# Own gate rows for the second chunk, four row transfers per later chunk, and a larger count for each junk matmul

## The chip, the cores and the metric

One core of one Trainium2 chip runs the whole program. The metric is the device time of one execution in microseconds (us). The kernel before took 325.11 us in the median of 3 runs (324.2 to 326.46). One more execution was recorded by the hardware profiler; it took 324.24 us by the same metric.

Engines are named as the profile names them: PE is the matmul engine (TensorE), PEld its weight loads, DVE is VectorE, ACT is ScalarE, POOL is GpSimd, SP is SyncE, which here only issues transfers. Each engine works through its own queue in order.

## What is computed

Three layers, one after another, on 2 batches of 768 steps. The first is a gated recurrent attention with 8 heads of 40 values, then a gated MLP that mixes along the sequence, then a channel mix.

```python
# 1: mLSTM, per batch b and head h, steps t = 0..767
m_new  = max(f[t] + m, i[t])
f_stab = exp(f[t] + m - m_new); i_stab = exp(i[t] - m_new); m = m_new
C = f_stab * C + i_stab * outer(v[t], k[t]);   n = f_stab * n + i_stab * k[t]
y[t] = sigmoid(o[t]) * (C @ q[t]) / max(|n . q[t]|, 1)
# 2: gMLP on x = y, 320 wide
h = relu(x @ w_in); u, v = h[:512], h[512:]
v_n = (v - mean(v)) / sqrt(var(v) + 1e-6)
x = (u * (w_spatial @ v_n + b_spatial)) @ w_out
# 3: channel mix on x, with xk, xr blends of x and x one step back
out = sigmoid(xr @ w_r) * (relu(xk @ w_k)**2 @ w_v)
```

## The kernel before

The recurrence is computed in chunks of 128 steps, 6 chunks in each of 2 batches, so 12 positions. `SEQ` orders them chunk by chunk: positions 0 and 1 are the first chunk of the two batches, 2 and 3 the second chunk, 4 and 5 the third, and so on. In text below "position 2" means the loop round p=2 as well as its chunk; the names of tasks stand in `position(p)` (L882 to L966).

For one position PE makes: the scores of q and k for both halves of the heads (`sc`, L458, task S0), the log decay matrix of each half (`ld`, tasks S0 and S1), the product of the earlier state with q (`ip`, L560, task I), the state update (`sp`, L526, task T), the weighted sum of values for each half (`av`, L580, tasks N0 and N1), and the turn of the result into columns (`tp`, L628, task X). ACT takes the exponential of `ld`, DVE multiplies it by the scores (`dt`), and DVE, POOL and ACT bring the result out as `x` and split it into a high and a low part (`xg`). The state update needs the weighted keys `kw` (POOL, L510), which need the position's key and value tile `kvq`.

Once a position is turned, its share of the gMLP's input product is queued as fillers: 8 matmuls of `vp` each (with `w_v`), and 32 of `up` (with `w_u`) for each pair of chunks of one batch. Fillers are a first-in, first-out list (`fill`, L781): if the head waits for its weights, nothing behind it is taken. The fillers of the first pair, positions 0 and 2, must be through before position 5 is turned, as only three `xg` tiles are kept (L621 to L623). `vp` goes through a normalisation chain (L717 to L723): relu on ACT, statistics on DVE, a root made of four small POOL operations (L712 to L715), the scaling on ACT (L722), then a high part on ACT and a low part on POOL (`vn`). The spatial mix (`spp`) reads all `vn`, and from there on come `wop`, `kp`, `rp` and `vv`.

**Gates.** The decays need running maxima `mg` and sums over each chunk. The first chunk's are computed at the start from the gate rows as they arrive, 16 rows of (batch, head) (`gate_set("a", 16, ...)`, L384 to L408, ten small operations; its tiles are `Lxa` and `Axa`). The remaining maxima are one scan of 640 columns (L810, called at L823). For all chunks together, `mg` and the gates are loaded again as 96 rows (`late_rows`, L836), the ten operations run on these (`gate_set("c", 96, ...)`, L847), and a task G at position 1 turns the result (`gpsc`, L415) and makes the state decays. The chunk sums are then moved by transfers into the operands `lt` and `rl` of the decay matmul (`gate_rows`, L421): 2 + 4 + 4 transfers for each chunk from the second on, the second chunk's at position 0. The first chunk's `ld` is made otherwise: `first_logd` (L462) uses `Lxa` and `Axa` where they lie, with six matmuls (L466, L468 four times, L470) instead of `ld` (L488) and its mask (L490).

**The order.** The program order of PE, ACT, DVE and POOL is laid down by a planner in the kernel while it is built: `clock[0]` is its time for PE, `free[...]` those of the other engines, chains are lists of (engine, cost, operation), and `load` keeps a due time for each transfer (230 KB per us up to 20 us, 360 after, plus 1.8 us). Where the next task isn't due, PE is given fillers, and where there is none, junk matmuls (`heat`, L350, tile `wp`), each counted at 0.107 us. So a planned wait becomes a fixed number of matmuls, whatever the chip does. Transfers are issued by SP in program order.

**Weights.** `w_in` comes in two halves, v and u, of three parts of 512 KB each, as 64-bit words, and is turned into two 32-bit tiles by a chain for each part (`widen`, L251: L273, L277, L281 on DVE, L272 and L289 on ACT, L233 on POOL). The v half is loaded before the loop. The u half is loaded whole at the end of position 0 (L940) and its chains are queued at position 1 (L889).

**Output gates.** ACT applies the sigmoid to the output gates of chunks 2 to 5 in task S1 of position 3 (L929); each change between sigmoid and exponential loads a table.

## Time and profile before

| | us |
|---|---|
| median of 3 runs (lowest, highest) | 325.11 (324.2, 326.46) |
| the profiled execution, same metric | 324.24 |
| its span from first to last instruction | 322.5 |
| mean granted TensorE clock, share of full speed | 0.993 |
| PE busy in the span | 308.0 |

A busy engine is one with an instruction under way; junk matmuls count as busy. Durations below are from the profiled execution. Its time stands 1.74 us above its span, and 0.87 us below the median of the timed runs. A row of the timeline gives start, duration, engine, line, operation, tile written and tiles read, shape and count; in brackets stands the idle time before it and what ended that.

### The profile page before, as it was taken

To read this page: it belongs to the slowest core of one execution; us is meant where nothing else is said; L and a number is where in the kernel's file an instruction comes from. 1 tells how busy PE (TensorE), PEld (TensorE's weight loads), DVE (VectorE), ACT (ScalarE), POOL (GpSimd) and SP (SyncE) were. 2 spreads that over 40 slices of the span, in tenths; PEclk is the share of its full clock that TensorE was granted. 3 is DMA by queue.
4 is the path that set the end of the run, shared out by engine and by line. 5 is a ranking of instruction groups with operands and counts; after the bars stand their busy time and mean duration, and the time that the engine had idled before them with its cause. 6 is when DMAs were issued, how large, how long until landed. Compare 5 with 4: busy or idle time off the path is not lost.

```text
span 322.5 us, 5694 instructions
## 1 busy us (share of the span) xinstructions
PE 308.0 (95%) x2075; PEld 286.9 (89%) x2075; DVE 211.3 (66%) x412; ACT 170.3 (53%) x354; POOL 155.0 (48%) x211
## 2 busy tenths in 40 slices
PE   7999989699999999977999999999999999999995
PEld 5866776689998998977999999999999999999995
DVE  7594496665655644463788998989866765645611
ACT  3631366754466555286334465476883754743610
POOL 5242167573575865377356652746722702502600
PEclk9999999899999999999999999999999999999999
DMA  6932946333424212204702520331101001001001
GB/s 164 294 87 80 321 140 192 109 109 104 152 87 153 92 31 69 89 25 130 229 20 74 170 86 24 92 114 40 42 2 62 0 22 41 2 20 41 2 20 41
DMA packets 14162, 28.78 MB, mean 89 GB/s; under 512 B 2567, under 2 KB 8007, under 8 KB 14135
## 3 DMA queue, kind: packets, MB, share of 16 engines
q1 hardware_dynamic: 14103, 28.37, 28.3%
q8 instruction: 16, 0.26, 0.3%
q0 software_dynamic: 32, 0.07, 0.1%
q14 instruction: 11, 0.09, 0.1%
HBM read 26.20 MB, written 1.97 MB: 87 GB/s over the span
## 4 chain that ended last, share of the span: by engine, by line
PE 77%; POOL 7%; DMA 5%; ACT 4%; DVE 3%; SPq 2%; issue 1%; DVEq 0%; POOLq 0%
PE spp L653 15%; PE kp L653 14%; PE vv L653 13%; PE wop L653 7%; PE wp L355 5%; PE vp L653 5%; PE rp L653 4%; PE up L653 4%; PE av L580 3%; PE sc L458 3%; DMA w_inv<-in_w_in_dram 2%; POOL vn L233 2%; PE ld L488 2%; SPq L214 2%; DMA kvq<-in_kvq_dram 1%
## 5 line engine op out<-in xcount | busy, mean ns | idle before, releaser
L1159 POOL TENSOR_TENSOR sq<-sq 128x384 f32<-128x384 f32 x32 | 29.9, 942 | 47.9 <-ACT sq L1158 47.8
L653 PE MATMUL spp<-wsp,vn 128*128 128x384 f32 x288 | 51.0, 335 | 1.7 <-POOL vn L233 1.3
L653 PEld LDWEIGHTS spp<-wsp,vn 128*128 128x128 f32 x288 | 49.8, 188 | 2.4 <-POOL vn L233 1.6
L653 PE MATMUL kp<-xk,wk 128*128 128x384 f32 x256 | 45.3, 334 | 0.0
L653 PEld LDWEIGHTS kp<-xk,wk 128*128 128x128 f32 x256 | 44.5, 188 | 0.0
L653 PE MATMUL vv<-wv,k 128*128 128x320 f32 x288 | 42.9, 309 | 0.0
L653 PEld LDWEIGHTS vv<-wv,k 128*128 128x128 f32 x288 | 42.4, 188 | 0.0
L233 DVE TENSOR_TENSOR k<-sq,k 128x384 fp32r<-128x384 f32 x32 | 26.1, 819 | 13.6 <-ACT k L1160 13.6
L653 PE MATMUL up<-xg,w_u 128*128 128x256 f32 x192 | 30.5, 293 | 2.3 <-ACT vr L718 1.4
L1056 POOL TENSOR_TENSOR vs<-vs,u 128x384 f32<-128x384 f32 x16 | 19.5, 1222 | 19.5 <-DVE vs L1055 18.1
L653 PEld LDWEIGHTS up<-xg,w_u 128*128 128x128 f32 x192 | 25.8, 191 | 3.4 <-ACT vr L718 1.6
L653 PE MATMUL vp<-w_v,xg 128*128 128x512 f32 x96 | 28.4, 411 | 0.0
L277 DVE SCALAR_TENSOR_TENSOR wbits<-wsq,wbits 128x320 int32<-128x320 int32 (+1 forms) x27 | 22.2, 822 | 8.7 <-ACT wsq L272 8.4
L580 PEld LDWEIGHTS av<-kvq,dt 128*128 128x128 f32 x192 | 25.2, 199 | 1.4 <-issue 0.3
L580 PE MATMUL av<-kvq,dt 128*128 128x123 f32 (+1 forms) x192 | 25.7, 279 | 0.3 <-DMA kvq<-in_kvq_dram 0.2
L1158 ACT ACTIVATE sq<-kp 128x384 f32<-128x384 f32 x32 | 15.5, 489 | 16.8 <-PE kp L653 14.8
L653 PE MATMUL wop<-gt,wo 128*128 128x384 f32 x128 | 22.8, 334 | 0.0
L653 PEld LDWEIGHTS wop<-gt,wo 128*128 128x128 f32 x128 | 22.2, 188 | 0.0
L501 DVE TENSOR_TENSOR dt<-dt,sc 128x512 f32<-128x512 f32 x20 | 13.6, 682 | 11.7 <-POOL dt L499 6.0
L233 POOL TENSOR_TENSOR vn<-vr,vn 128x512 fp32r<-128x512 f32 x12 | 16.3, 1355 | 7.3 <-ACT vn L723 7.3
L498 ACT ACTIVATE dt<-ld 128x512 f32<-128x512 f32 x20 | 11.9, 597 | 14.7 <-PE ld L490 7.6
L653 PEld LDWEIGHTS vp<-w_v,xg 128*128 128x128 f32 x96 | 17.3, 189 | 2.6
(160 smaller groups left out, 575.6 us busy)
## 6 DMA issues: line engine op xcount, KB each, us to landing
kvq<-in_kvq_dram SPq DMA_DIRECT2D x10, 516.0 KB
qk<-in_qk_dram SPq DMA_DIRECT2D x24, 160.0 KB
wraw<-in_w_k_dram SPq DMA_DIRECT2D x6, 512.0 KB
wraw<-in_w_v_dram SPq DMA_DIRECT2D x8, 320.0 KB
wraw<-in_w_sp_dram SPq DMA_DIRECT2D x12, 192.0 KB
og<-in_o_tok_dram SPq DMA_DIRECT2D x12, 160.0 KB
out_dram<-ob SPq DMA_DIRECT2D x12, 160.0 KB
w_inv<-in_w_in_dram SPq DMA_DIRECT2D x3, 512.0 KB
```

Source lines behind the costliest of these rows:

```text
L214: sync.dma_start(out=out, in_=in_)
L233: eng.tensor_tensor(out=out, in0=a, in1=b.bitcast(F32), op=ALU.subtract)
L277: vec.scalar_tensor_tensor(out=t["bits"], in0=t["sq"].bitcast(I32), scalar=3, in1=t["bits"], op0=ALU.logical_shift_left, op1=ALU.bitwise_or)
L355: pe.matmul(wp[:, :256], junk[:, :P], junk, start=True, stop=True)
L458: pe.matmul(st["sc", i, x][:, h * P:(h + 1) * P], k_[64 * x:64 * x + D, h, :], q_[64 * x:64 * x + D, h, :], start=True, stop=True)
L498: ("A", 0.48, lambda: act.activation(out=d2, in_=ld, func=AF.Exp), ("e", i, hh)),
L501: ("V", 0.6, lambda: vec.tensor_tensor(out=d2, in0=d2, in1=sc, op=ALU.mult)))
L580: pe.matmul(av[:, own_, :], A[:, h, :], vt[:, own_, :], start=True, stop=True)
L653: pe.matmul(out[0], l, x, start=j == 0, stop=j == len(prs) - 1)
L1056: ("P", 1.29, lambda: pool.tensor_tensor(out=vs, in0=vs, in1=ut[b][:, d, sl], op=ALU.mult)),
L1158: chain(("k2", g, f), ("A", 0.49, lambda: act.activation(out=sq, in_=ps, func=AF.Relu), ("kp", g, f)), ("P", 0.96, lambda: pool.tensor_ten ...
L1159: ("P", 0.96, lambda: pool.tensor_tensor(out=sq, in0=sq, in1=sq, op=ALU.mult)),
```

## The change

- The second chunk gets a gate set of its own on the 16 rows as they lie (`gate_set("b", 16, ...)`), and its `ld` is made by `first_logd` as the first chunk's. The scan is cut in three: the first chunk, the second, and the last four (512 columns).
- The 96-row set is loaded and computed later: its loads come after the q and k of position 2, its chain is due from 20 us at the earliest, and task G moves from position 1 to position 2. A new task B at position 0 turns the second chunk's gates.
- `gate_rows` begins with the third chunk, at position 2. It makes 2 + 2 transfers for each chunk instead of 2 + 4 + 4; odd and even chunks use different rows of `rl`, and both halves are written at once, in task S0.
- A junk matmul in a wait is counted at 0.187 us instead of 0.107.
- The u half of `w_in` is loaded one part at each of positions 0, 1 and 2, and its chains are queued at position 3.
- For positions from the sixth on, the normalisation leaves out two of the four POOL operations and scales on DVE instead of ACT.
- The transfers ahead of the loop are put in another order: position 1's `kvq` before the second part of the v half, the q and k of position 2 before the late rows.

```diff
     def idle_to(t):
         while warm[0] and clock[0] < t - 0.1:
             heat(1)
+            clock[0] += 0.08
             advance(clock[0])
...
-    first_ = {k: gp.tile([P, P], F32R, name=k + "xa") for k in "LA"}
+    first_ = {(k, nm): gp.tile([P, P], F32R, name=k + "x" + nm) for nm in "ab" for k in "LA"}
...
-            for first, sign in ((-16, 1), (17, -1)):
+            for first, sign in ((-16 - 4 * j, 1), (17 + 4 * j, -1)):
...
-    def gate_rows(c, hh):
-
+    def gate_rows(c):
         finish(("G1", 0), stall=False)
         after = done["G1", 0]
         L, A = [G1[k][c:96:NCH] for k in "LA"]
-        if hh == 0:
-            for b in range(B):
-                load(lts[c % 2][:16, b].bitcast(F32), A[8 * b:8 * b + 8].rearrange("h w t -> h (w t)").bitcast(F32), 8, after)
+        for b in range(B):
+            load(lts[c % 2][:16, b].bitcast(F32), A[8 * b:8 * b + 8].rearrange("h w t -> h (w t)").bitcast(F32), 8, after)
         for w in range(2):
-            for b in range(B):
-                r = 16 + 2 * b + w
-                e = load(rl[r:r + 1, 512 * hh:512 * hh + 512].bitcast(F32),
-                         L[8 * b + 4 * hh:8 * b + 4 * hh + 4, w].bitcast(F32), 2, after)
+            r = 16 + 4 * (c % 2) + w
+            e = load(rl[r:r + 3:2, :].bitcast(F32), L[:, w].bitcast(F32), 8, after)
...
     def egate(b, c, w):
-        if c < 1:
+        if c < 2:
             return GC[c]["eg"][:, w, 8 * b:8 * b + 8]
...
     def logd(i, hh):
         b, c = divmod(i, NCH)
-        if c == 0:
+        if c < 2:
+            if ("A", i, hh) not in st:
+                first_logd(i, hh)
             sc = st.pop(("sc", i, hh))
...
-        early = SEQ.index(i) < 4
-        pe.matmul(ld, lts[c % 2][:, b], rl[:, hh * 512:(hh + 1) * 512], start=True, stop=not early)
-        if early:
-            pe.matmul(ld, mask[:, 1], mask[:, 0:1].to_broadcast([P, 4, P]), start=False, stop=True)
-            clock[0] += 0.21
+        pe.matmul(ld, lts[c % 2][:, b], rl[:, hh * 512:(hh + 1) * 512], start=True, stop=True)
...
+            early = SEQ.index(i) < 5
+
             def root():
                 pool.tensor_tensor(out=sb[:, 8:9], in0=sb[:, 7:8], in1=eps[:, 0:1], op=ALU.add)
                 pool.tensor_tensor(out=sb[:, 8:9], in0=sb[:, 8:9], in1=eps[:, 1:2], op=ALU.pow)
+                if not early:
+                    return
...
-                  ("P", 1.2, root),
-                  ("A", 0.6, lambda: act.activation(out=vr, in_=vr, func=AF.Identity, scale=sb[:, 8:9], bias=sb[:, 9:10])),
+                  ("P", 1.2 if early else 0.75, root),
+                  ("A", 0.6, lambda: act.activation(out=vr, in_=vr, func=AF.Identity, scale=sb[:, 8:9], bias=sb[:, 9:10]))
+                  if early else
+                  ("V", 0.46, lambda: vec.tensor_scalar(out=vr, in0=vr, scalar1=sb[:, 6:7], scalar2=sb[:, 8:9],
+                                                        op0=ALU.subtract, op1=ALU.mult)),
...
             elif warm[0] and gap > 0.2:
                 heat(1)
+                clock[0] += 0.08
                 advance(clock[0])
...
-    scan(1, NCH)
-    free["V"] = 8.7
+    GC[1], late_steps = chunk_gates(1)
+    free["V"] = 7.0
...
-    for a in 'k0 v0 q6 v1 r k6 v2 b e'.split():
-        dict(k=lambda: load_kv(SEQ[a != "k0"]), q=lambda: load_qk(SEQ[1]), r=late_rows,
+    for a in 'k0 v0 q6 k6 v1 b v2 n'.split():
+        dict(k=lambda: load_kv(SEQ[a != "k0"]), q=lambda: load_qk(SEQ[1]), n=lambda: load_qk(SEQ[2]),
...
-    G1, steps = gate_set("c", 96, f2, i2, m2[:, 0], m2[:, 1], vec, act.copy)
-    ...
-    chain(("G1", 0), *[(e, dict(V=0.3, A=0.3)[e], f) for e, f in zip('VVVVAVVAVVV', steps)], ready=st["late"])
+    chain(("G0", 1), ("V", 0.26, lambda: scan(1, 2)), *[("V", 0.28, f) for f in late_steps], ready=6.9)
...
-    load_qk(SEQ[2])
+    finish(("G0", 1), stall=False)
+    chain(("G0", 2), ("V", 1.3, lambda: scan(2, NCH)))
+    finish(("G0", 2), stall=False)
+    late_rows()
+    for t, x in ((ex_sb, expand), (pk_sb, pick)):
+        load(t, x, 48)
+    G1, steps = gate_set("c", 96, f2, i2, m2[:, 0], m2[:, 1], vec, act.copy)
+    ...
+    chain(("G1", 0), *[(e, dict(V=0.3, A=0.3)[e], f) for e, f in zip('VVVVAVVAVVV', steps)], ready=max(st["late"], 20.0))
...
-            if p == 1:
+            if p == 3:
                 w_in_split("u")
...
-            if p % 2 == 0 and p + 2 < NT:
-                gate_rows(p // 2 + 1, 0)
+            if p % 2 == 0 and 2 <= p < NT - 2:
+                gate_rows(p // 2 + 1)
...
-            if p % 2 == 0 and p + 2 < NT:
-                gate_rows(p // 2 + 1, 1)
...
             if p == 0:
-                w_in_load("u", 0, 0, 1, 2)
+                w_in_load("u", 0, 0)
                 sync.dma_start(out=mu_sb, in_=mu)
             if p == 1:
+                w_in_load("u", 0, 1)
...
             if p == 2:
+                w_in_load("u", 0, 2)
...
-        if p == 1:
+        if p == 0:
+            task("B", lambda: (wait(("G0", 1)), gate_exp("b", 16, GC[1])), [("G0", 1)], slot=7, p=p)
+        if p == 2:
             task("G", gates, [("G1", 0)], p=p, slot=7)
...
-                task(("T", i), st_, [("kw", i)], [("I", i), ("N1", prev)] + ["G"] * (p >= 1), slot=2, p=p)
+                task(("T", i), st_, [("kw", i)], [("I", i), ("N1", prev)] + ["G"] * (p >= 2), slot=2, p=p)
```

## Rows read from the trace of the kernel before

**Rows 1.** The page's first part: busy us, share of the span, instructions.

```profile
PE 308.0 (95%) x2075; PEld 286.9 (89%) x2075; DVE 211.3 (66%) x412; ACT 170.3 (53%) x354; POOL 155.0 (48%) x211
```

**Rows 2.** Windows: stretch and length, busy us of each engine, clock, DMA share, GB/s.

```profile
17.30:27.20 9.90, 9.90 (x64) 6.19 (x65) 8.35 (x22) 2.81 (x7) 4.88 (x6) 1.00 0.15 43
27.20:36.40 9.20, 9.20 (x71) 6.61 (x69) 3.35 (x10) 2.55 (x7) 1.39 (x2) 1.00 0.66 215
36.40:50.15 13.75, 12.89 (x101) 10.68 (x100) 11.09 (x28) 7.27 (x17) 7.14 (x13) 1.00 0.61 198
73.95:126.60 52.65, 52.01 (x425) 47.74 (x425) 30.08 (x85) 28.72 (x65) 33.57 (x59) 1.00 0.32 100
126.60:148.94 22.34, 18.80 (x116) 16.46 (x114) 9.88 (x22) 13.20 (x30) 12.76 (x27) 1.00 0.29 89
148.94:322.50 173.56, 170.20 (x1039) 169.94 (x1039) 121.63 (x181) 90.01 (x182) 71.71 (x68) 1.00 0.18 55
```

**Rows 3.** Windows of the junk tile wp alone: PE busy, count, clock, DMA.

```profile
17.30:27.20 9.90, 8.96 (x56) 1.00 0.15 43
27.20:36.40 9.20, 3.72 (x22) 1.00 0.66 215
36.40:50.15 13.75, 2.54 (x15) 1.00 0.61 198
50.15:56.57 6.42, 1.69 (x7) 1.00 0.56 183
```

**Rows 4.** Timeline, 17 to 35 us: PE, DVE, SP and POOL around the first wait.

```profile
17.28 1.12 PE L580 MATMUL av<-kvq,dt 128*128 128x123 f32 x8 [0.23 <-DMA kvq<-in_kvq_dram]
18.24 9.16 PE L355 MATMUL wp<-id_sb 128*128 128x256 bf16 x56
...
22.08 1.54 SPq L214 DMA_DIRECT2D lt<-Axc  x2
...
23.34 0.23 DVE L848 TENSOR_SCALAR lpk<-pk_sb,f 96x36 f32<-96x36 f32 x1
...
29.88 0.38 SPq L214 DMA_DIRECT2D kvq<-in_kvq_dram  x1
...
34.09 0.74 POOL L510 TENSOR_TENSOR kw<-kvq,egc 128x320 f32<-128x320 f32 x1 [7.60 <-DMA kvq<-in_kvq_dram]
```

**Rows 5.** Timeline: position 4's scores, the first up filler, the last w_u step.

```profile
50.15 1.16 PE L458 MATMUL sc<-qk 40*128 40x128 f32 x16
...
69.68 0.37 PE L653 MATMUL up<-xg,w_u 128*128 128x256 f32 x1
...
69.96 1.53 POOL L233 TENSOR_TENSOR w_u<-wsq,w_u 128x512 fp32r<-128x512 f32 x1
```

**Rows 6.** Timeline, 7 to 13 us: the long scan, and two first_logd starts.

```profile
7.21 1.53 DVE L810 TENSOR_TENSOR_SCAN mg<-fg,mg,ig 16x640 f32<-16x640 f32 x1
...
11.50 0.48 PE L466 MATMUL ld<-unit,Axa 128*128 128x512 f32 x1
...
12.26 0.57 PE L466 MATMUL ld<-unit,Axa 128*128 128x512 f32 x1
```

**Rows 7.** Chain that ended last, 33 us: ld and its mask (start, us).

```profile
33.50 0.42 PE ld L488
33.92 0.23 PE ld L490
```

**Rows 8.** Tile w_inu: two DVE steps of w_u's widening, ns min/median/max.

```profile
L273 DVE TENSOR_SCALAR wbits<-w_inu x3: 418/420/894, 37.0 to 54.7; 128x512 int32<-128x512 int32 x3
L281 DVE SCALAR_TENSOR_TENSOR wsq<-w_inu,wbits x3: 658/680/1631, 47.3 to 63.8; 128x512 int32<-128x512 int32 x3
```

**Rows 9.** Timeline at 61 us: PE's wait behind the sigmoids.

```profile
61.14 0.81 PE L526 MATMUL sp<-kvq,kw 128*120 128x123 f32 x6 [2.35 <-ACT dt L498]
```

**Rows 10.** Windows of one us: the granted clock after that wait.

```profile
62.00:63.00 1.00, 0.97 (x4) 0.97 (x5) 1.00 (x4) 0.78 (x3) 0.66 (x2) 0.50 0.43 127
```

**Rows 11.** Line 722: ACT's scaling in the normalisation, ns min/median/max.

```profile
L722 ACT ACTIVATE vr<-vr,sb x12: 799/816/819, 42.6 to 147.7; 128x512 f32<-128x512 f32 x12
```

More of the change, by code (lines that the diff above doesn't have):

```diff
@@ L359, in tile_mlstm_gmlp_channelmix @@
     vec.memset(unit.bitcast(F32), 0.0)
-    for k in "LA":
-        vec.memset(first_[k].bitcast(F32), 0.0)
+    for t in first_.values():
+        vec.memset(t.bitcast(F32), 0.0)
     for a in 'f i d o0 o1 q'.split():
@@ L391, in gate_set @@
             if R == 16:
-                g[k + "h"], g[k + "l"] = first_[k][:16], first_[k][32:48]
+                g[k + "h"], g[k + "l"] = first_[k, nm][:16], first_[k, nm][32:48]
             else:
@@ L462, in first_logd @@
     def first_logd(i, hh):
-        r0 = 8 * (i // NCH) + 4 * hh
+        r0, nm = 8 * (i // NCH) + 4 * hh, "ab"[i % NCH]
         ld = bank(psa, "at", f"ld{i}_{hh}", ("e", i, hh))
-        pe.matmul(ld, first_["A"], unit[:, r0:r0 + 4].unsqueeze(2).to_broadcast([P, 4, P]), start=True, stop=False)
+        pe.matmul(ld, first_["A", nm], unit[:, r0:r0 + 4].unsqueeze(2).to_broadcast([P, 4, P]), start=True, stop=False)
         for h in range(4):
-            pe.matmul(ld[:, h * P:(h + 1) * P], unit[:, r0 + h:r0 + h + 1].to_broadcast([P, P]), first_["L"],
+            pe.matmul(ld[:, h * P:(h + 1) * P], unit[:, r0 + h:r0 + h + 1].to_broadcast([P, P]), first_["L", nm],
                       start=False, stop=False)
@@ L498, in logd @@
               ("A", 0.48, lambda: act.activation(out=d2, in_=ld, func=AF.Exp), ("e", i, hh)),
-              *[] if early else [("P", 0.59, lambda: pool.affine_select(out=dt, in_=dt, compare_op=ALU.is_ge, fill=0.0, base=0,
-                                                     pattern=[[0, 4], [1, P]], channel_multiplier=-1))],
+              ("P", 0.59, lambda: pool.affine_select(out=dt, in_=dt, compare_op=ALU.is_ge, fill=0.0, base=0,
+                                                     pattern=[[0, 4], [1, P]], channel_multiplier=-1)),
               ("V", 0.6, lambda: vec.tensor_tensor(out=d2, in0=d2, in1=sc, op=ALU.mult)))
@@ L563, in inter @@
         beat(0.57)
-        finish(("eg", "c"), stall=False)
+        finish(("eg", "abc"[min(c, 2)]), stall=False)
         chain(("nn", i), ("V", 0.41, lambda: vec.tensor_tensor(
@@ L839, in late_rows @@
         for w in range(2):
-            st["late"] = load(m2[:, w], mg[:, w:w + S], 48, 8.7)
-    for a in 'k0 v0 q6 v1 r k6 v2 b e'.split():
-        dict(k=lambda: load_kv(SEQ[a != "k0"]), q=lambda: load_qk(SEQ[1]), r=late_rows,
-             v=lambda: w_in_load("v", 1, int(a[1])), b=lambda: load(bm_raw, blockmask[:, 0:3 * DA:DA], 2),
-             e=lambda: [load(t, x, 48) for t, x in ((ex_sb, expand), (pk_sb, pick))])[a[0]]()
+            st["late"] = load(m2[:, w], mg[:, w:w + S], 48, 14.0)
+    for a in 'k0 v0 q6 k6 v1 b v2 n'.split():
+        dict(k=lambda: load_kv(SEQ[a != "k0"]), q=lambda: load_qk(SEQ[1]), n=lambda: load_qk(SEQ[2]),
+             v=lambda: w_in_load("v", 1, int(a[1])), b=lambda: load(bm_raw, blockmask[:, 0:3 * DA:DA], 2))[a[0]]()
     w_in_split("v", hv)
-    G1, steps = gate_set("c", 96, f2, i2, m2[:, 0], m2[:, 1], vec, act.copy)
-    steps.append(lambda: vec.tensor_scalar(out=lpk, in0=pk_sb, scalar1=G1["Lc"][:, P - 1:P], scalar2=None, op0=ALU.mult))
-    chain(("G1", 0), *[(e, dict(V=0.3, A=0.3)[e], f) for e, f in zip('VVVVAVVAVVV', steps)], ready=st["late"])
+    chain(("G0", 1), ("V", 0.26, lambda: scan(1, 2)), *[("V", 0.28, f) for f in late_steps], ready=6.9)
     heat(36)
@@ L854, in tile_mlstm_gmlp_channelmix @@
         first_logd(SEQ[0], x)
-        st["rows", SEQ[0], x] = st["rows", SEQ[1], x] = 0.0
+        for i in SEQ[:4]:
+            st["rows", i, x] = 0.0
     heat(4)
@@ L865, in tile_mlstm_gmlp_channelmix @@
         first_logd(SEQ[1], x)
-    load_qk(SEQ[2])
+    finish(("G0", 1), stall=False)
[5 more added lines that the diff above has]
+    G1, steps = gate_set("c", 96, f2, i2, m2[:, 0], m2[:, 1], vec, act.copy)
+    steps.append(lambda: vec.tensor_scalar(out=lpk, in0=pk_sb, scalar1=G1["Lc"][:, P - 1:P], scalar2=None, op0=ALU.mult))
+    chain(("G1", 0), *[(e, dict(V=0.3, A=0.3)[e], f) for e, f in zip('VVVVAVVAVVV', steps)], ready=max(st["late"], 20.0))
     def decays():
@@ L993, in tile_mlstm_gmlp_channelmix @@
                 heat(1)
+                clock[0] += 0.08
                 advance(clock[0])
```

9 lines of the change are left out of this document (5 added, 4 removed).

## The prediction

> **What bounds the kernel now.** I read the busy shares first. PE is busy for 95% of the span, no other engine for more than 66% [rows 1]. That alone would say that only less matmul work can help. But a junk matmul counts as busy, so the next view is the windows by stage, beside the same windows for the junk tile alone. From 148.94 us to the end PE works 170.20 of 173.56 us, and the change touches nothing there. From 73.95 to 126.60 us it works 52.01 of 52.65 us; here too PE is the bound, as it is fed by a stock of fillers [rows 2]. Both stretches just start earlier or later. What can move is what lies ahead of 73.95 us, and a little in 126.60 to 148.94, where PE stands 3.54 us of 22.34.
>
> The windows of the junk tile show where the early time goes: 8.96 us in 17.30 to 27.20, 3.72 to 36.40, 2.54 to 50.15, 1.69 to 56.57, in all 16.9 us in which a busy PE does nothing [rows 3].
>
> The timeline then says what it waits for. After the `av` of position 1 at 17.28 come 56 junk matmuls in one block of 9.16 us. They stand for task G: the turn of the 96-row gates and the decays. The last gate operation, `lpk`, ends at 23.34 + 0.23 = 23.57 us, yet the block runs to 27.40 [rows 4]. The planner counted 56 x 0.107 = 6.0 us, and the chip took 56 x 0.160 = 8.96. So some 6 us of the block are a true wait for gates, the rest is junk that runs past its cause. The row transfers of the second chunk come behind it: SP begins with them at 22.08 us and only reaches the `kvq` of position 2 at 29.88, so that its `kw` starts at 34.09 after POOL stood 7.60 us [rows 4]. That is why more junk stands up to 36.40.
>
> **The change, part by part.** The sum is made against the profiled execution's 324.24 us.
>
> *First wait.* Positions 2 and 3 no longer need the 96 rows, so neither their `ld` nor the state update of position 1 waits for G. What is late next is the q and k of position 2. By the planner's own due times (2.2 us, then 230 KB per us in the new order of the transfers, plus 1.8) they are due at 21.1 us. PE has some 1 to 2 us of work until then (the turn of the gates, the state update of position 1, perhaps the turn of position 0). From 18.3 us, the end of that `av` [rows 4], about 1.7 us stay open; at 0.187 us counted that is 9 junk matmuls, 9 x 0.160 = 1.4 us. I take -7.5 us of the 8.96; the bounds are -6 (all of 18.3 to 21.1 junk) and -8.96.
>
> *Second wait.* The 3.72 us of junk in 27.20 to 36.40 stand for rows of the second chunk that no longer travel: -3.7, at worst 0 if the `kvq` of position 2 is as late as now. It shouldn't be: on SP it stands behind late rows, two small loads and one position's q and k, and no longer behind ten row transfers that wait for the gates. The scan must end before the `mg` rows can go, which I put at about 16 us; then `kvq` goes out near 19 us instead of 29.88, and even with the 4.2 us that it took to `kw` [rows 4] arrives by 24.
>
> *Less junk in the remaining waits.* 22 junk matmuls stand in 36.40 to 56.57, 4.23 us [rows 3]. At 0.187 for 0.107 a planned wait gets 57% of them: -1.8. Zero, if what is waited for comes no earlier than now.
>
> *Added on PE.* A half by `first_logd` takes 12.26 - 11.50 = 0.76 us [rows 6], one by `ld` and mask 0.42 + 0.23 = 0.65 [rows 7]: four halves, +0.4, and the two small turns of the new gates +0.3. Together +0.7; bounds 0.4 and 1.2.
>
> *Added on DVE.* The new gate set is a short scan and ten operations like those of the first chunk, and the long scan is cut from 640 to 512 columns, 1.53 x 512/640 = 1.2 us [rows 6]. The gates run while PE is in its planned start-up junk, but the scan now stands after them, among the first part of the v weights: up to 1.2 us of DVE delay before 17.3 us. The two more cleared tiles run before the gates arrive and cost nothing.
>
> *Rows of later chunks.* Four transfers instead of ten free SP, but from 73.95 us on PE never waits for SP, so 0. One new wait: the `ld` of the second half in positions 4, 6 and 8 reads all rows of `rl`, and so waits for the rows that the first task of that position has just sent for the next chunk. PE, ACT's `dt` and all fillers behind it would wait. In positions 6 and 8 several us of fillers stand between, which hides it; without them it would be up to 1.3 us each time. In position 4, which has none, I take +1.0 (0 to 1.3).
>
> *Normalisation.* For seven positions ACT's scaling of 0.816 us [rows 11] and two POOL operations go, and a DVE operation comes, which I put between 0.42 and 0.68 us, as the one- and two-tensor operations on the same shape [rows 8]. In 73.95 to 126.60 PE covers it all, and DVE has 22 us free there [rows 2]. Only at the end could a shorter chain tell, in the 3.54 us of standing; bounds -2 and +1, taken 0.
>
> Sum: -7.5 - 3.7 - 1.8 + 0.7 + 1.0 = -11.3 us.
>
> *The other engine.* With PE's waits gone, DVE is next. From 17.30 to 50.15 us, where position 4's scores start [rows 5], it is busy for 8.35 + 3.35 + 11.09 = 22.8 us [rows 2]. About 3.4 us of that widen u weights (two parts, each 0.42 + 2 x 0.68 [rows 8]), which now comes later; 1.2 us of scan is pushed in. So some 20.6 us of DVE work must pass before the same point. With DVE never idle position 4 starts at 37.9 us, 12.2 earlier; at the 84% that DVE reached in its best window here (8.35 of 9.90) at 41.8, 8.3 earlier. The sum of -11.3 lies between. I take -10.3, the middle.
>
> *The u weights.* Their chains now begin at position 3, just ahead of the eight sigmoids on ACT, through which each part must pass twice. Today they end at 69.96 + 1.53 = 71.5, and the first `up` starts at 69.68 [rows 5]; until then the head of the filler list blocks everything behind it, and PE lives on position work alone. Position work will be some 10 us earlier, the u weights probably less. I charge +0.8 us of standing for it, between 0 and the 2.35 us that PE stood behind the sigmoids [rows 9].
>
> Together -9.5 us: 324.24 - 9.5 = 314.7 for an execution like the profiled one. The median lies 0.87 above that one, so 315.5 us.
>
> *A rule against it.* After PE had stood 2.35 us behind the sigmoids [rows 9], the granted clock was 0.50, that is 1.2 GHz, in three windows of 1 us (62 to 65) [rows 10]; while PE is kept on junk it stays at 1.00 [rows 3]. So such a wait costs its 2.35 us and half of 3 us more, 3.85 in all. The Trainium skill, "TensorE: Matmul & The Clock Gate", section "HAM oscillation — how this bites in real kernels", says that waits in which the matmul engine idles make the gate throttle again each time, and this row agrees with it. By that rule removing junk is no saving where the wait stays. My sum keeps the junk for 0.160/0.187 = 86% of each planned wait, so it adds no event; by the rule every wait that outlasts its plan would add one.
>
> **The rivals.**
> - *DVE or the u weights bind early.* DVE gets no better than its 13.75 us window (11.09, 81%) and stands behind ACT as well, or `w_u` ends near 65 us, so that the filler list is blocked through position 5. Then 3 to 7 us are gained: 318 to 322. For it: 8.35 of 9.90 us of DVE busy [rows 2]. Against it: part of that is statistics and weight work that can wait.
> - *The clock.* Real waits outlast the thinner junk, and PE idles. Two such events of 3.85 us leave 9.5 - 7.7 = 1.8 us: 323.3, no change that can be told. For it: one event stands in the trace already. Against it: the largest wait goes altogether.
> - *The u weights stop the loop* (slower). Position 5 can't be turned before the `up` of the first pair is through. If `w_u` takes from position 4's start, at about 40 us, as long as it takes now from the end of the first wait, 27.40 [rows 4], to 71.5, that is 44 us, it ends at 84, 12.5 later than now. Being 10 us ahead, PE has about 6 us of position matmuls more behind it by then (my estimate, from the share of its busy time in 36.40 to 50.15 that isn't junk or `vp`); it then runs dry, and the end comes 12.5 - 6 = 6.5 us later than now: 331.6. It decides from where `w_u` ends after 77.5 us. Against it: the raw parts come earlier in relation to the split, and DVE has less beside them.
> - *More than forecast.* DVE hides it all, and the shorter normalisation gives 2 us at the end: 13 to 16 us, 309 to 312.
>
> **How the numbers follow.** Forecast (312 to 318) 0.48; DVE or weights bind (318 to 322) 0.20; clock, no change, 0.14; u weights stop the loop 0.08; more than forecast 0.10. A change of under 1%, 3.25 us, can't be told from none here; so faster is below 321.9. Faster 0.48 + 0.20 + 0.10 = 0.78, same 0.14, slower 0.08. The range 309 to 322.5 leaves out the slower rival, most of the clock's, and the far end of the last: about 0.2. The likeliest case alone is 312 to 318.
>
> **What would show it.** Right: the block of 56 junk matmuls is gone, with under 15 before position 2's scores; these start near 21 us; `kw` of position 2 before 25; position 4's scores at 38 to 42 (now 50.15); junk in all under 8 us; PE dense from about 64 us. Wrong: DVE above 90% in 17 to 40 us with PE standing behind `dt` or `xg`; a clock of 0.50 in more than one place; the first `up` later than 65 us; PE standing at `ld` behind a transfer of rows; standing in the tail that grows beyond 3.54 us.

## The result, and the profile after

The changed kernel takes 313.08 us (median of 3 runs, 312.19 to 313.5) where the kernel before took 325.11: a ratio of 0.9621, interval 0.9557 to 0.9684. That is faster by 12.0 us; forecast were 315.5 us and a range of 309 to 322.5. The profiled execution of the new kernel took 313.5 us, its span 311.8.

The whole difference of the spans can be accounted for in two views, the windows from 17.30 us to the end and the same windows of the junk tile. Columns as in [rows 2] and [rows 3]. The kernel before:

```profile
17.30:322.50 305.20, 293.29 (x1955) 274.56 (x1955) 199.96 (x384) 161.55 (x339) 147.45 (x193) 0.99 0.26 81
17.30:322.50 305.20, 16.92 (x97) 0.99 0.26 81
```

The kernel after, first the page's first part, then these two windows and some stretches of its own:

```profile
PE 298.6 (96%) x2010; PEld 283.4 (91%) x2010; DVE 220.8 (71%) x432; ACT 165.6 (53%) x348; POOL 153.5 (49%) x197
...
17.30:311.80 294.50, 283.60 (x1891) 271.00 (x1889) 207.01 (x392) 157.26 (x332) 147.65 (x179) 0.98 0.27 84
17.30:311.80 294.50, 2.55 (x14) 0.98 0.27 84
...
17.30:36.34 19.04, 18.69 (x147) 15.25 (x145) 16.69 (x46) 10.49 (x25) 9.58 (x13) 1.00 0.71 222
36.34:62.17 25.83, 20.72 (x150) 17.75 (x149) 20.29 (x46) 18.37 (x38) 20.68 (x28) 0.87 0.50 164
55.08:61.90 6.82, 5.24 (x21) 4.57 (x22) 5.98 (x12) 3.48 (x9) 6.77 (x8) 0.50 0.32 101
72.00:115.00 43.00, 43.00 (x351) 39.58 (x350) 27.93 (x75) 22.93 (x51) 29.96 (x48) 1.00 0.34 100
115.00:140.00 25.00, 23.43 (x139) 21.41 (x138) 15.71 (x31) 12.11 (x29) 14.54 (x22) 0.94 0.21 65
```

Before, PE's 305.20 us were 16.92 of junk, 305.20 - 293.29 = 11.91 of standing and 276.37 of other work. After, the 294.50 us are 2.55 of junk, 10.90 of standing and 281.05 of other work. So junk fell by 14.4 us, standing by 1.0, and the other work grew by 4.7 us; together 10.7, the difference of the spans. By the prediction's estimate the change adds about 0.7 us of matmuls. Some 2.7 us are the same matmuls at the lower clock: 0.50 (1.2 GHz) from about 55.1 to 61.9 us with 5.24 us of work, and again from 137.0 to about 140.4 us with 3.4, where before there was one such stretch with 3.4 us of work, round [rows 10]; half of 5.24 + 3.4 - 3.4 is 2.6 to 2.7. I can't place the last 1.3 us.

The timeline of after shows where the gain begins and where a part of it seems to be given back (start, us, engine, line, operation; in brackets the idle time before it and its releaser):

```profile
18.29 0.71 PE L356 MATMUL wp<-id_sb 128*128 128x256 bf16 x4
19.84 1.57 PE L356 MATMUL wp<-id_sb 128*128 128x256 bf16 x9
21.34 1.16 PE L456 MATMUL sc<-qk 40*128 40x128 f32 x16
...
27.88 0.72 POOL L506 TENSOR_TENSOR kw<-kvq,egb 128x320 f32<-128x320 f32 x1
...
36.34 1.16 PE L456 MATMUL sc<-qk 40*128 40x128 f32 x16
...
53.15 2.50 POOL L234 TENSOR_TENSOR w_u<-wsq,w_u 128x512 fp32r<-128x512 f32 x2
53.23 0.81 ACT L722 ACTIVATE vr<-vr,sb 128x512 f32<-128x512 f32 x1 [1.09 <-POOL sb L715]
54.45 0.67 ACT L273 ACTIVATE wsq<-w_inu 128x512 f32<-128x512 f32 x1 [0.40 <-POOL w_u L234]
55.90 0.60 ACT L494 ACTIVATE dt<-ld 128x512 f32<-128x512 f32 x1
56.55 0.80 PE L487 MATMUL ld<-rl,lt 128*128 128x512 f32 x1 [2.80 <-ACT dt L494]
60.92 1.26 POOL L234 TENSOR_TENSOR w_u<-wsq,w_u 128x512 fp32r<-128x512 f32 x1
62.17 0.37 PE L649 MATMUL up<-xg,w_u 128*128 128x256 f32 x1
```

The block of 56 junk matmuls of [rows 4] has become 13, in two pieces. Position 2's scores start at 21.34 us, those of position 4 at 36.34, 13.8 us earlier than in [rows 5]. But the first `up` starts at 62.17, only 7.5 us earlier, in the moment in which the last `w_u` part is ready (60.92 + 1.26 = 62.18). Ahead of it PE stands 5.1 us in 36.34 to 62.17; the longest wait is 2.80 us for an exponential. That one was late because ACT works in order: in front of it stood a scaling that waited for POOL's `sb`, and a weight step that waited for POOL's `w_u`.

The first `up` doesn't tell how much work is left. Another mark does: behind the start of the last block of `vp`, eight matmuls, the same 1098 matmuls are left in every kernel here. The windows from this mark to the end, in the kernel before, the kernel after, and the first part of the change alone (e4_core, below):

```profile
135.81:322.50 186.69, 179.79 (x1098) 178.14 (x1096) 126.71 (x190) 99.83 (x204) 81.50 (x85) 1.00 0.18 56
125.52:311.80 186.28, 180.84 (x1098) 179.60 (x1096) 129.04 (x193) 97.29 (x200) 79.92 (x80) 0.99 0.18 57
123.80:305.80 182.00, 178.69 (x1098) 178.09 (x1096) 126.89 (x191) 99.14 (x203) 80.17 (x84) 1.00 0.18 59
```

At the mark the new kernel is 10.3 us ahead of the kernel before, at the end 10.7. The gain is neither the 13.8 us at position 4 nor the 7.5 us at the first `up`.

### The profile page after: what moved, and what is told of

The parts are those of the page before. It is cut to its first block, busy times and chain, and to the rows that moved or that the text cites. A ratio compares the mean times of both kernels' runs of the same rounds, so it can differ in the third digit from the quotient of the medians.

```text
span 311.8 us, 5519 instructions
## 1 busy us (share of the span) xinstructions
PE 298.6 (96%) x2010; PEld 283.4 (91%) x2010; DVE 220.8 (71%) x432; ACT 165.6 (53%) x348; POOL 153.5 (49%) x197
## 4 chain that ended last, share of the span: by engine, by line
PE 80%; DVE 6%; ACT 4%; POOL 4%; issue 2%; DMA 1%; SPq 1%; DVEq 0%; ACTq 0%; POOLq 0%
PE spp L649 16%; PE kp L649 14%; PE vv L649 14%; PE wop L649 7%; PE up L649 6%; PE vp L649 5%; PE rp L649 5%; PE av L576 4%; PE sc L456 2%; PE ip L556 2%; PE sp L522 2%; PE ld L487 1%; DMA og<-in_o_tok_dram 1%; POOL vn L234 1%; PE tp L624 1%
## 5 line engine op out<-in xcount | busy, mean ns | idle before, releaser
L649 PE MATMUL spp<-wsp,vn 128*128 128x384 f32 x288 | 52.6, 342 | 1.6 <-ACT vn L726 0.8
L649 PEld LDWEIGHTS spp<-wsp,vn 128*128 128x128 f32 x288 | 51.4, 193 | 2.2 <-ACT vn L726 1.2
L649 PE MATMUL up<-xg,w_u 128*128 128x256 f32 x192 | 29.2, 291 | 0.0
L1212 DVE TENSOR_TENSOR ob<-rs,vv 128x320 f32<-128x320 f32 x12 | 5.8, 487 | 19.7 <-PE vv L649 18.7
L282 DVE SCALAR_TENSOR_TENSOR wsq<-wraw,wbits 128x320 int32<-128x320 int32 (+1 forms) x21 | 18.2, 870 | 0.3
```

What stands on the lines that cost most here:

```text
L282: vec.scalar_tensor_tensor(out=t["sq"].bitcast(I32), in0=t["high"], scalar=SIGN, in1=t["bits"], op0=ALU.bitwise_and, op1=ALU.bitwise_or)
L649: pe.matmul(out[0], l, x, start=j == 0, stop=j == len(prs) - 1)
L1212: vec.tensor_tensor(out=ob, in0=rs, in1=ps, op=ALU.mult)
```

## Experiments

Each time is the median of 4 executions (10 for e8_before_heat187); the ratio is to the kernel before on the same chip (medians 324.3 to 325.5 us). "The whole change" is the kernel after. In each, the planner makes its order anew, so the order of other work can move with the edit; where it did, that is said.

**The first part alone** (e4_core). The second chunk keeps its own gates, and the new order of the start; the other four parts are put back.

```
-  clock[0] += 0.08                       (junk counted 0.107 again)
-  early = SEQ.index(i) < 5               (ACT scales in every position)
+  early = True
-  gate_rows(c): four transfers           (ten again)
-  if p == 3: w_in_split("u")             (u loaded whole, split at 1)
+  if p == 1: w_in_split("u")
```

> Only the second chunk's own gates with what belongs to them (scan in three parts, task B, G at position 2, late rows and the order of the first transfers); the count of junk, the u half, the normalisation and the 2 + 4 + 4 row transfers (from the third chunk on) as before the change. Theory (the first two waits are the gain): 8 to 11 us under the kernel before, 314 to 317 us, junk of the first wait under 25 matmuls. Rival (the parts need each other, as DVE is full with u in the same stretch): 318 to 322 us.

308.13 us, ratio 0.9479 (0.9415 to 0.9544), 5 us less than the whole change, and 6 below the band that was expected. Windows, timeline:

```profile
17.30:305.80 288.50, 281.36 (x1909) 268.71 (x1907) 201.97 (x384) 162.30 (x339) 147.92 (x193) 1.00 0.27 85
17.30:305.80 288.50, 6.21 (x33) 1.00 0.27 85
115.00:140.00 25.00, 25.00 (x157) 23.74 (x157) 13.21 (x28) 15.29 (x33) 16.24 (x30) 1.00 0.27 80
...
42.08 1.16 PE L459 MATMUL sc<-qk 40*128 40x128 f32 x16
50.38 0.72 PE L652 MATMUL up<-xg,w_u 128*128 128x256 f32 x4
54.01 1.28 POOL L234 TENSOR_TENSOR w_u<-wsq,w_u 128x512 fp32r<-128x512 f32 x1
```

It has more junk than the whole change (33 against 14) and reaches position 4 nearly 6 us later (42.08 against 36.34), and still ends 6.0 us earlier by span: its `w_u` is ready at 55.29 instead of 62.18, its first `up` starts 11.8 us earlier, it stands 7.1 us instead of 10.9, and in the profiled execution the clock never falls. So the gain is that of this one part, and the other four together cost 5 us. By the mark, 1.7 of the 6.0 us arise ahead of the last `vp` (123.80 against 125.52) and 4.3 behind it, where e4_core stands 3.31 us instead of 5.44 and is busy 2.15 us less with the same matmuls, mostly as its clock doesn't fall there. So the wait for `w_u` at 62.18 us itself explains 1.7 us of the difference at most.

**Less junk per wait**, tried three times: the whole change with the old count (e1_heat107), the kernel before with the new count (e8_before_heat187), and the first part with the new count (e12_core_heat187). The edit is the one line in three places, put in for the last two and taken out for the first:

```
+  clock[0] += 0.08
```

> The changed kernel with each junk matmul in a wait counted at 0.107 us again; all else as changed. Theory (little is left to save, as the large waits are gone): after the start the changed kernel has 14 junk matmuls, 2.2 us; at 0.107 they become about 24, so +1.6 us, 314 to 315 us. Rival (the larger count was worth what the prediction gave it and keeps the planner in step): +3 or more, 316 or later. Rival (the clock): more junk keeps the granted clock at 1.00 round 55 us, and the time is the same or shorter, 311 to 313.

313.28 us, ratio 0.9624 (0.9568 to 0.9679), with 22 junk matmuls for 14: nothing. The theory's 314 to 315 was too high.

> The kernel before with one part of the change: a junk matmul in a wait counted at 0.187 us. Theory of the prediction (a planned wait gets 57% of the junk, and where the block ran past its cause that is saved): the block of 56 becomes about 32, 5.1 us instead of 9.0, and ends near the last gate operation; with the later waits 4 to 7 us are gained, 318 to 321.5 us. Rival (the row transfers behind the gates bind, not the junk): 324 to 326 us.

327.84 us, ratio 1.0073 (1.0041 to 1.0105): a little slower, and above both bands that were expected. The junk falls from 97 to 58, the big block ends at 24.4 us instead of 27.40, and the scores of position 4 still start at 50.13 us. Junk is 6.5 us less (10.45 for 16.92) and standing 7.1 us more (18.99 for 11.91). One such wait is for the rows of the second chunk; others are for `xg` and `kw`:

```profile
18.87 5.50 PE L356 MATMUL wp<-id_sb 128*128 128x256 bf16 x33
...
28.69 0.47 PE L489 MATMUL ld<-rl,lt 128*128 128x512 f32 x1 [1.55 <-DMA rl<-Lxc]
...
50.13 1.16 PE L459 MATMUL sc<-qk 40*128 40x128 f32 x16
```

> Only the second chunk's own gates, plus the planner's count of 0.187 us for a junk matmul. The order on ACT keeps the sigmoids where they were. Theory (junk is not what costs: what PE waits for comes no earlier): fewer junk matmuls, 33 now to some 15, and the same time, 307.6 to 309. Prediction's step (a planned wait gets 57% of the junk and ends earlier): 1 to 1.8 us less, 306.3 to 307.2. Rival (thinner junk lets the clock fall in the waits): above 309.5 with a clock under 0.9 in some stretch of 20 to 60 us.

307.4 us, ratio 0.9461 (0.9419 to 0.9503), with 21 junk matmuls for 33. That is 0.2 us under the theory's band and 0.7 below e4_core, inside the spread of either (306.77 to 308.41, 307.55 to 310.3). Here the clock did fall, as the rival said, though not at the rival's price:

```profile
49.66:56.48 6.82, 6.11 (x31) 5.85 (x29) 3.56 (x9) 4.81 (x10) 3.85 (x9) 0.50 0.18 54
```

e4_core never fell, and both reach the last `vp` at 123.80 us. Up to there e12_core_heat187 has 2.1 us less junk and 0.4 less standing, and 2.5 us more of other busy time: what the junk freed went into slower matmuls. The one execution of it with a mean clock of 1.00 took 306.77 us, the two such of e4_core 307.55 and 307.73. In none of the three kernels did junk taken away come back as time by the medians. In e8_before_heat187 it only showed the wait that lay under it.

**The clock** (e5_warm). The whole change with 18 junk matmuls put into the wait of 2.80 us, order otherwise the same:

```
   idle_to(st["rows", i, hh])
+  if (i, hh) == (SEQ[6], 0): heat(18)    (put in other words; not counted in the planner's clock)
```

> The changed kernel with 18 junk matmuls more and no other difference in any queue: they stand ahead of the ld of position 6's first half, where PE stood 2.80 us behind ACT, after which the granted clock was 0.50 from 55 to 61.5 us. Theory (the u weights bind there: w_u is finished on POOL at 62.18 us, and up starts at 62.17): the clock stays at 1.00, PE only waits longer for w_u, gain under 1 us, 312.3 to 313.3 us. Rival (the clock's fall is the price): half of some 6 us comes back, 310 to 310.5 us.

312.62 us, ratio 0.9595 (0.9549 to 0.9641), against 313.08: 0.5 us, which can't be told from nothing. The clock stayed at 1.00 up to 59 us and was low for only some 3.4 us instead of 6.8 (1.00 throughout was expected), and yet the first `up` starts at 62.32. In the profiled execution the second fall, at 137 us, is missing too:

```profile
58.00:59.00 1.00, 0.23 (x3) 0.09 (x2) 0.94 (x3) 0.30 (x1) 1.00 (x2) 1.00 0.01 2
137.00:138.00 1.00, 1.00 (x8) 1.00 (x7) 0.27 (x1) 0.76 (x3) 0.92 (x3) 1.00 0.24 25
...
62.32 0.47 PE L649 MATMUL up<-xg,w_u 128*128 128x256 f32 x1
```

So the first fall seems hidden up to the first `up`: while PE works at half speed, the u weights are late anyhow. But of the four executions the one with a mean clock of 1.00 took 310.88 us, near the rival's 310 to 310.5, and the others, at 0.992 to 0.995, 312.44 to 313.14. It is a single one without a trace, so that the falls are free isn't shown. The trace shows them hidden only up to there: in e10_vn_act_wo_late (below) the clock was 0.50 until 64 us, past the first `up` at 62.29.

**The u weights** (e2_u_early, e6_core_u_late): the whole change with the u half of w_in loaded whole and split at position 1, as before; and the first part with u sent by position and split at 3.

```
-  if p == 3: w_in_split("u")
+  if p == 1: w_in_split("u")
-  p == 0: w_in_load("u", 0, 0);  p == 1: w_in_load("u", 0, 1);  p == 2: w_in_load("u", 0, 2)
+  p == 0: w_in_load("u", 0, 0, 1, 2)
```

This is the edit of e2_u_early; e6_core_u_late has it the other way round.

> The changed kernel with the u half of w_in loaded whole at position 0 and its chains queued at position 1, as before the change. Theory (late u weights cost PE its fillers): the first up comes well ahead of 62 us, PE no longer stands in 52 to 57 us, and the time is 308 to 311 us. Rival (DVE is full in 17 to 40 us, so that the chains of u push the position work back there): position 4's scores come 2 us or more after 36.3, 314 to 316 us.

312.5 us, ratio 0.9602 (0.9546 to 0.9659): no more than 0.6 us, where 308 to 311 us were expected. The first `up` does start earlier, at 57.8 us, but the planner now puts the block of sigmoids (a table load of 1.28 us, eight sigmoids in 2.98, a table load of 1.28) on ACT ahead of both exponentials of position 4:

```profile
44.67 1.28 ACT L348 ACT_TABLE_LOAD   x1
45.97 2.98 ACT L348 ACTIVATE og<-og 128x320 f32<-128x320 f32 x8
...
50.81 0.60 ACT L494 ACTIVATE dt<-ld 128x512 f32<-128x512 f32 x1
51.46 0.80 PE L456 MATMUL sc<-qk 40*128 40x128 f32 x4 [6.61 <-ACT dt L494]
```

> The second chunk's own gates as in the run before with them alone (308.13 us), plus one part of the change: the u half loaded by position and its chains queued at position 3. Theory (the late u weights are what takes back the gain of reaching position 4 sooner): first up at 60 us or later instead of 50.4, a stretch at clock 0.50, and 311.5 to 314 us. Rival (another part, or the mere order of ACT's queue round the sigmoids): within 1.5 us of 308.1.

316.5 us, ratio 0.9751 (0.9686 to 0.9816): 8.4 us more than without it, and more than the 311.5 to 314 expected. Nor did the other sign come: the first `up` starts at 52.06, not after 60. What it costs stands elsewhere. By spans it is 9.1 us, 3.8 ahead of the last `vp` (127.58 us) and 5.3 behind it. Ahead, PE stands 2.4 us more in 36 to 64 us, and the clock was 0.76 in 50 to 64 us. Behind, ACT's queue is blocked by a cast of w_out's first part. That cast writes into a page that the last `vp` still reads, and the steps of the normalisation stand behind it:

```profile
129.39 0.46 ACT L290 CAST wo<-wsq 128x320 fp32r<-128x320 f32 x1 [4.98 <-PE vp L652]
...
115.00:140.00 25.00, 21.41 (x136) 19.00 (x134) 11.20 (x25) 13.88 (x32) 14.01 (x28) 1.00 0.16 49
```

**Rows in four transfers** (e11_core_rows4), added to the first part:

```
-  10 loads: lts by b; rl by (w, b, hh), 1 row of 4 heads each
+  4 loads: lts by b; rl by w, rows 16 + 4*(c % 2) + w and + 2, all heads
```

> Only the second chunk's own gates, plus the later rows in four transfers. Seen beforehand in the order of the instructions: with four transfers the planner puts the eight sigmoids on ACT ahead of both exponentials of position 4 and not between them. Theory (the price of this part is not its transfers but that order): PE stands 2 to 6 us behind dt in 40 to 56 us and the time is 309.5 to 312 (308.13 without it); no wait of an ld on a row transfer is longer than 0.5 us. Rival (the rows part is worth nothing or a little either way, as the prediction had from 73.95 us on): 307.5 to 308.7.

317.72 us, ratio 0.978 (0.9747 to 0.9813): 9.6 us more than e4_core, where 1.4 to 3.9 were expected. The transfers aren't waited for: no `ld` waits for one longer than 0.5 us. By spans the cost is 10.0 us, 5.8 ahead of the last `vp` (129.55 us) and 4.2 behind it. What the trace shows ahead of it is the order on ACT. As in e2_u_early, the sigmoids stand ahead of both exponentials of position 4 (in e4_core they stand between them, after 44.50), PE stands 6.60 us, and the clock is at 0.50 for some 13 us. Behind the last `vp` the cast for w_out waits again, 4.58 us. No run puts the order back with the four transfers kept, so this cause is read from the trace and not tested:

```profile
44.00:48.00 4.00, 0.46 (x2) 0.29 (x2) 1.00 (x4) 3.97 (x8) 1.53 (x3) 0.62 0.64 183
48.00:52.00 4.00, 0.50 (x4) 0.50 (x6) 1.38 (x2) 3.97 (x8) 0.48 (x1) 0.50 0.15 54
...
46.01 2.98 ACT L348 ACTIVATE og<-og 128x320 f32<-128x320 f32 x8
...
50.85 0.60 ACT L494 ACTIVATE dt<-ld 128x512 f32<-128x512 f32 x1
51.50 2.08 PE L456 MATMUL sc<-qk 40*128 40x128 f32 x14 [6.60 <-ACT dt L494]
```

**The normalisation** (e3_vn_act, e7_core_vn_dve): the whole change with ACT's scaling in all positions, and the first part with DVE's scaling in the last seven.

```
-  early = SEQ.index(i) < 5
+  early = True
```

> The changed kernel with the normalisation of all positions on ACT and with four POOL operations, as before the change. Theory (covered by PE's work, only the end could tell): 312.5 to 314 us. Rival (the shorter chain is worth its latency at the end, where spp waits for vn): +1 to +2.5, 314 to 315.5 us.

317.67 us, ratio 0.9753 (0.9685 to 0.9822): 4.6 us more, above both bands that were expected. So in the whole change the DVE scaling is worth 4.6 us.

> The second chunk's own gates alone, plus one part of the change: the scaling of the normalisation on DVE from the sixth position on. Theory (covered by PE where the end is dense, as it is in the run with the gates alone): 307.5 to 308.7 us. Rival (it is worth what it was in the whole change, 4.6 us): 303 to 305 us. Rival (DVE gets a load that it has no room for): 310 or more.

309.53 us, ratio 0.9512 (0.9483 to 0.9541): 1.4 us more than e4_core, at the edge of what these runs can tell (one execution of e4_core took 310.3). There it gains nothing at least. In its trace the cast for w_out waits 2.12 us, and PE stands 1.01 us in 115 to 140, where in e4_core it doesn't stand. The difference called for a reason. In e3_vn_act the tail looks like that of e6_core_u_late, with the same cast ahead of the normalisation:

```profile
115.00:140.00 25.00, 20.47 (x128) 18.07 (x127) 10.88 (x25) 13.92 (x33) 14.39 (x28) 1.00 0.20 58
...
128.44 0.46 ACT L290 CAST wo<-wsq 128x320 fp32r<-128x320 f32 x1 [4.98 <-PE vp L649]
...
138.35 0.62 PE L649 MATMUL spp<-wsp,vn 128*128 128x384 f32 x2 [1.66 <-ACT vn L726]
140.42 9.82 PE L649 MATMUL spp<-wsp,vn 128*128 128x384 f32 x46 [1.45 <-POOL vn L234]
```

In e4_core the same casts run at 125.92 us and later without a wait for `vp`.

**The cast at the end of the loop** (e9_wo_late, e10_vn_act_wo_late). The widening of w_out's first weights is moved behind sixteen more fillers, in the whole change and in e3_vn_act:

```
+  closing.append(0)
+  fill(16)
   for j in range(4):
       widen("w_o", ...)
-  closing.append(0)
   fill(len(fillers) + len(later))
```

> The whole change with the normalisation as before (ACT scales) and the same move of w_out's widening behind sixteen filler steps. Without the move this normalisation cost 4.6 us more (317.67). Theory (its ACT step was only dear because it stood in ACT's queue behind the cast that waits for the last vp): the 4.6 us shrink to 1.5 at most, 311.5 to 314.5. Rival (the chain of the normalisation itself is too long for the end of the loop, whatever stands ahead of it): still 3 us or more above the kernel with the DVE scaling, 315 to 317.5.

313.92 us, ratio 0.9653 (0.9617 to 0.9688), where 317.67 and 0.9753 stood without the move: 3.75 us less by the medians, 3.3 by the ratios, as the two ran on different chips. The theory held: most of the 4.6 us that the ACT scaling cost hung on the cast in front of it. Beside e9_wo_late, with the same move on the same chip, ACT's scaling costs nothing that can be told (313.92 against 314.4). The cast now has no wait, and PE stands 0.47 us in 115 to 140 us instead of 4.53:

```profile
115.00:140.00 25.00, 24.53 (x157) 22.98 (x158) 11.74 (x25) 15.85 (x35) 15.97 (x30) 1.00 0.17 48
...
129.74 0.48 ACT L290 CAST wo<-wsq 128x320 fp32r<-128x320 f32 x1
```

> The whole change, with one thing moved: the widening of w_out's first weights is put behind sixteen more steps of the filler list, so that its casts on ACT come after the relu of the last vp and no longer ahead of it. Theory (the tail is made by ACT's queue: a cast waits for the last vp to read the page it overwrites, with the normalisation's steps behind it): PE's standing in 115 to 140 us, 1.57 us now, falls under 0.5, the cast's wait of 4.77 us on ACT goes or comes under 1, and the time is 311 to 312.5. Rival (the cast has slack and the tail is set by DVE and POOL): no change, 312.8 to 313.5.

314.4 us, ratio 0.9678 (0.9625 to 0.973): no gain, and the spread is wide, 313.07 to 316.16. The wait did go, PE is busy for 25.00 of 25.00 us in 115 to 140. But then the matmuls wait for the spatial weights, which now come behind:

```profile
115.00:140.00 25.00, 25.00 (x162) 23.62 (x161) 16.15 (x31) 11.55 (x28) 13.13 (x19) 1.00 0.16 49
...
147.34 0.80 PE L649 MATMUL spp<-wsp,vn 128*128 128x384 f32 x3 [0.67 <-DVE wsp L234]
148.62 1.69 PE L649 MATMUL spp<-wsp,vn 128*128 128x384 f32 x8 [0.49 <-DVE wsp L234]
```

Its profiled execution is the slowest of the four (316.16), so the missing gain is read from the times, and only the new wait from this trace. With the DVE scaling 1.57 us of standing were left to win, and a new standing of 1.16 takes their place. The theory had the wait right and the time wrong.

**Where each run gains and loses.** From the profiled executions: the mark, the time from it to the end, and how long the first cast for w_out waits for `vp`.

| | last `vp` starts | from there to the end | the cast waits |
|---|---|---|---|
| before | 135.81 | 186.69 | 4.98 |
| e8_before_heat187 | 136.54 | 188.96 | 4.98 |
| after | 125.52 | 186.28 | 4.77 |
| e1_heat107 | 125.29 | 186.21 | 4.77 |
| e5_warm | 125.77 | 184.93 | 4.77 |
| e3_vn_act | 126.62 | 189.38 | 4.98 |
| e2_u_early | 127.96 | 182.54 | 1.05 |
| e4_core | 123.80 | 182.00 | no |
| e12_core_heat187 | 123.80 | 182.10 | no |
| e7_core_vn_dve | 124.06 | 183.94 | 2.12 |
| e11_core_rows4 | 129.55 | 186.25 | 4.58 |
| e6_core_u_late | 127.58 | 187.32 | 4.98 |
| e10_vn_act_wo_late | 127.69 | 184.81 | no (moved) |
| e9_wo_late | 126.61 | 187.79 | no (moved) |

In the kernels with the cast in its place, the end takes 182.0 to 182.5 us where it waits a little or not at all, 183.9 at 2.12 us, and 184.9 to 189.4 where it waits for 4.5 or more. That the cast is the cause was tried only by moving it: in e3_vn_act's kernel 4.6 us of the end went with the wait, in the whole change another wait came in its place. Falls of the clock lie in the same stretch in some of these runs.

## Why the prediction was right, and where it was not

The time came out 2.4 us below the forecast, inside the likeliest case (312 to 318). The mechanism named for the first two waits is the one that the runs show. That the sum came out so near was luck. In the forecast the whole -9.5 us is the first part of the change (-7.5, -3.7, +0.7, and +1.0 for DVE), and the other four parts come to nothing (-1.8, +1.0, +0.8 and 0). Measured are -17.4 us for the first part and +5.0 for the other four: two misses, of nearly 8 and of 5 us, in opposite directions.

*First and second wait* (-7.5 and -3.7): right in mechanism and in the junk, too small in the time. Junk in all of 17.30 us to the end fell by 14.4 us. Forecast was under 8 us of junk left; 2.55 us are. In e4_core, where the count is as before, junk fell by 10.7 us (16.92 to 6.21) for the 11.2 forecast. Position 2's scores were expected near 21, and start at 21.34. One mark was missed: position 2's `kw`, expected before 25 us, starts at 27.88. No gain seems to hang on it, since position 3's scores start at 27.17 without it. e4_core shows that the part that takes these waits away is the whole gain: 17.4 us for it alone, by the medians on that chip (325.52 to 308.13). Its spans differ by 16.7: beside the 10.7 us of junk, 4.8 us are standing that went (11.91 to 7.14) and 1.2 other busy time. By the mark, 12.0 us are gained ahead of the last `vp` and 4.7 behind it, in a stretch in which the prediction allowed for 2 us at most, and that from another part, the normalisation. There the cast for w_out waited 4.98 us before and doesn't in e4_core; no run on the kernel before tried whether that is why.

*Less junk in the remaining waits* (-1.8): this term was wrong. Three kernels give 0, a loss of 0.7% and 0. A junk matmul too many is only lost if what PE waits for is there already. In the waits of [rows 3] it was not: e8_before_heat187 lost 6.5 us of junk and gained 7.1 of standing. The prediction had that case as its other bound (zero) and chose the wrong end. In e12_core_heat187 the clock fell as well, so there the two effects can't be told apart.

*DVE as the next bound* (-10.3 instead of -11.3): the bound doesn't stand where I put it. I counted 20.6 us of DVE work ahead of position 4's scores and so set them at 37.9 to 41.8 us. They came at 36.34, with 16.69 us of DVE work done by then. The rest ran after them, so it wasn't all needed first. (The term also has a slip: two u parts at 0.42 + 2 x 0.68 are 3.6 us, not 3.4.) DVE was indeed busy for 16.69 of 19.04 us, but PE did not stand behind it.

*The u weights* (+0.8): undersized; by how much depends on the rest. Of the 13.8 us gained up to position 4 only 7.5 are left at the first `up`. Its wait on `w_u` at 62.18 us, with PE standing 5.1 us ahead of it, is what the prediction's first rival described, though that gave 318 to 322 us and the time was less. At the last `vp` 10.3 us are left, 1.7 fewer than in e4_core. The price of sending u by position alone is +8.4 us (e6_core_u_late), over half of it behind the last `vp`. Loading it early in the whole change gives back only 0.6: by the mark 2.4 us are lost ahead of it, where the sigmoids take its place, and 3.7 gained behind it. So the same step costs between 0.6 and 8.4 us, depending on what ACT does next.

*Rows of later chunks* (+1.0 for one wait, else 0): the wait didn't come. No `ld` stands behind a row transfer in the whole change. What came instead was not in the prediction at all: by itself this part costs 9.6 us. Some 5.8 of it go with the order on ACT and 4.2 with the end of the loop, as far as one trace shows. In the whole change the sigmoids stand between position 4's exponentials again (37.97 and 48.22 us). Why the planner orders them so in one kernel and not in the other I didn't follow; it rests on its modelled times.

*Normalisation* (0, bounds -2 and +1): as a single number this was wrong both ways, 4.6 us gained in the whole change, nothing or a loss of 1.4 on the first part alone, nothing where the cast is moved. "PE covers it" holds until the loop's end. There, whether it tells hangs on ACT's queue: when the cast for w_out stands ahead of it, waiting for the last `vp`, the step that no longer runs on ACT is worth several us. That cast was there before the change as well, as ACT's timeline of the kernel before shows:

```profile
137.63 0.46 ACT L289 CAST wo<-wsq 128x320 fp32r<-128x320 f32 x1 [4.98 <-PE vp L653]
```

It may be behind the 3.54 us of standing in 126.60 to 148.94 [rows 2], for which the prediction named no cause; on the kernel before that wasn't tried. In e4_core, with the same scaling and no such wait, PE doesn't stand in 115 to 140 us.

*The clock* (rival, 323.3): one of the prediction's signs of being wrong came, a clock of 0.50 in more than one place. The granted clock fell twice, in the wait of 2.80 us and after 0.84 + 0.73 us of standing. The Trainium skill, "TensorE: Matmul & The Clock Gate", section "HAM oscillation — how this bites in real kernels", says that waits make the gate throttle again, and the trace agrees as to that. The price was not 3.85 us each: cutting the first low stretch to half and losing the second brought 0.5 us by the medians (e5_warm). The one execution of that kernel with a mean clock of 1.00 was 2.2 us below the median of the whole change, so both together may have cost about that; this isn't shown.

*The sum of the parts.* On the first part, the other four alone give -0.7 (count), +1.4 (normalisation), +8.4 (u) and +9.6 (rows), in sum +18.7; all four together give +5.0. They don't add. Each can change the order in which ACT gets its work, and that is the likely reason. The prediction added its terms, and was near because the first part gained more than forecast by about as much as the others cost. The fastest kernels measured here are e4_core and e12_core_heat187, at 308.13 and 307.4 us, which can't be told apart.

## What to carry to other kernels

Removing what the largest wait is for (here, gates of 96 rows ahead of two positions that need 16) saves an amount of filler that can be sized from the trace (10.7 us for 11.2 forecast), though not what follows from it (17.4 us in all); taking filler out of a wait without removing its cause gained nothing in three tries. When the first wait goes, look at what else had been timed against it: here PE's next wait ended with weights that had been moved later at the same time, and behind the loop a cast in another engine's queue made as much difference. Compare kernels at a mark behind which all have the same work left; an earlier mark can mislead. Try the parts of a change singly: on an engine that works in order, a block of 5.5 us or a cast that waits for a page decides more than any part's own instructions.

## What the runs showed of the hardware

- An in-order engine turns one wait into many. A cast of 0.46 us on ACT that waited 4.98 us for a page held up the normalisation behind it; moved, it gave 3.3 to 3.75 us back (e3_vn_act against e10_vn_act_wo_late).
- Eight sigmoids cost ACT 2.98 us, but with the two table loads of 1.28 us around them they bar it to exponentials for 5.5 us, and PE stood 6.60 us when its exponentials came behind (e11_core_rows4).
- Time at the low clock is not lost one for one: e12_core_heat187, 6.8 us at 0.50, and e4_core, never below 1.00, reach the last `vp` at the same 123.80 us. What the slower matmuls take in the first, 2.5 us, e4_core spends on more junk and standing.
